# Turning exponentials with unit-matrix matmuls and the state by DMA, in an attention and Fourier-mix kernel

## The chip, the cores and the metric

The kernel runs on one core of one Trainium2 chip. The metric is device time in microseconds of one execution, measured several times; a profile of one execution shows where the time goes.

PE is the matmul engine (PEld its weight loads), DVE the vector engine, ACT the scalar engine, POOL is GpSimd, SP the sync engine whose queue issues most DMAs.

## The reference, cut to what matters

```python
# x: (8, 8, 512, 64) = batch, head, row, d;   state: (8, 8, 32, 64)
scores  = x @ state.T / 8;   a  = softmax(scores);   xread = a @ state      # 512 rows per head
scores2 = state @ x.T / 8;   a2 = softmax(scores2);  sread = a2 @ x         # 32 rows per head
attn    = concat([xread, sread], axis=2)            # 544 rows; heads are laid side by side
mixed   = real(fft over rows, then over d_model)    # 544 x 512 per batch
u       = attn + mixed
out     = u + relu(layer_norm(u) @ w_ch1) @ w_ch2   # 512 -> 2048 -> 512
```

The two score matrices are transposes of each other. The kernel needs their exponentials in two layouts: E has rows of x on partitions and feeds the state's reads; ET has states on partitions and feeds the reads of x. (The softmax goes without subtracting the maximum; the sums come from columns of ones.)

## The kernel before

A batch runs in three stages that are woven with those of its neighbours. In stage b the two MLP layers of batches b and b-1 give PE its bulk; batch b+1 makes its reads and its Fourier transform, and batch b+2 its scores. The parts that the change touches:

```python
def load_state(lo, hi):                    # partitions: (head of 4, state)
    nc.sync.dma_start(out=stf[:, lo:hi]..., in_=state[lo:hi].rearrange("b (g hh) j d -> (hh j) (b g) d", hh=4))

load_state(0, 1); load_x(0); load_state(1, B); load_x(1)

def more_loads():                          # on GpSimd, in this order
    ...
    nc.gpsimd.tensor_tensor(gate, xs_of[0][:, :, 0], w1[:, :, 3 * 512], op=ALU.add)
    load_x(2)                              # SP queue, follows the gate
    state_blocks(2, B, nc.gpsimd.tensor_copy)        # spreads the state of batches 2 to 7 into stb
    nc.gpsimd.tensor_copy(gate, xs_of[2][:, :, 0])   # waits for x of batch 2
    for q in range(4):
        nc.gpsimd.dma_start(out=w2[...], in_=w2v[...])   # second weights
# ---- cut ----
def turn_state():                          # sT = the state with d on partitions
    p = qt("sTp", BF16)
    for pr in range(4):
        g, hp = pr // 2, pr % 2
        nc.tensor.transpose(p[:, pr * 128:(pr + 1) * 128], sb[:, g, 4 + 128 * hp:132 + 128 * hp], ident)
    nc.vector.tensor_copy(sT, p[:, 0:512]...)        # ScalarE for batches 0 and 1

def scores_t(g):                           # states on partitions
    p = qt("eTp")
    for lo, hi, src in ((0, NM, slice(0, NM)), (NM, S, slice(S - 1, NM - 1, -1))):   # NM = 288, S = 512
        for hp in range(2):
            nc.tensor.matmul(p[:, lo:hi], lhsT=sT[:, 2 * g + hp, :], rhs=xT[:, 2 * g + hp, src], ...)
    nc.scalar.activation(ET[:, g, :], p, AF.Exp, scale=scale)

def scores(i):                             # rows on partitions, 64 columns per matmul, state backwards
    ...
    nc.scalar.activation(E[:, 2 * i:2 * i + 2]..., p, AF.Exp, scale=scale)

def fold_early():                          # batches 0 and 1 only: part of the fold on GpSimd
    fold_low(True, nc.gpsimd); next(fold_rows(slice(0, 1), nc.gpsimd)); fold_low(False, nc.gpsimd)
def fold():                                # the rest on VectorE, ending in the four XQ
    ...
# ---- cut: from batch 3 on x is turned by DMA; the order of a batch's score steps is ----
first = ([] if b >= x_by_dma else [turn_state, turn_x 0, turn_x 1]) + [scores_t(0), scores_t(1), scores(0), scores(1)]
# from batch 3 on turn_state stands first
```

The softmax here doesn't subtract the row's maximum and nothing guards it: scores larger than these inputs give would overflow.

## Time and profile before

| | before |
|---|---|
| time, median of 4 runs | 323.83 us (323.62 to 323.89) |
| span of the profiled execution | 322.0 us |
| PE / DVE / ACT / POOL busy | 95 / 59 / 45 / 22 % |
| PE busy from 80 to 260 us | 99.1 % |

The prediction below shows the views that say what bounds the kernel. First, two groups that the change removes, from the list of groups (line, engine, operation, tiles, shapes, count, then busy us, mean ns, idle time before and what ended it):

```profile
L362 PE MATMUL eTp<-xT,sT 128*128 128x288 bf16 (+1 forms) x64 | 9.6, 273 | 0.1
...
L338 DVE COPY sT<-sTp 128x512 bf16<-128x512 bf16 x6 | 2.5, 425 | 14.3 <-PE sTp L337 14.3
```

The 273 ns of a score matmul is its time from start to end. Matmuls overlap in the pipeline, so its price on a busy PE is read from the chain in order of time (0.44 us for four), not from this mean.

Second, GpSimd between 30 and 51 us, from its timeline (start, length, instruction):

```profile
30.77 3.42 POOL L147 CAST stb<-gen 32x768 bf16<-32x768 f32 x4
34.26 0.26 POOL L294 COPY gate<-xs 128x4 f32<-128x4 f32 x1
34.47 3.04 POOL L296 DMA_DIRECT2D w<-in_moe_w_ch_dram  x4
...
43.21 0.66 POOL L427 TENSOR_TENSOR XE<-XL 32x256 f32<-32x256 bf16 x1 [2.23 <-DVE XL L399]
...
46.20 0.72 POOL L430 TENSOR_TENSOR XO<-XL 32x255 f32<-32x255 bf16 x1
50.34 0.19 POOL L735 CAST gate<-XQ 128x1 f32<-128x1 bf16 x1 [3.42 <-DVE XQ L451]
```

It spreads the state, issues the second weights, and does its part of batch 1's fold (sums and differences of mirrored rows, called Sm, XE, XO and XQ, which the Fourier transform takes as input), for which it waits 2.23 us. At 50.34 us it passes the gate (a small copy made only to wait for something) behind which it casts x of batch 2. Third, two of VectorE's steps in the same fold, a sum Sm and the first XQ:

```profile
45.95 0.45 DVE L434 TENSOR_TENSOR Sm<-XF,XR 128x514 bf16<-128x514 bf16 x1
...
47.38 0.56 DVE L446 TENSOR_TENSOR XQ<-XE 128x384 bf16<-128x384 f32 x1
```

### The profile page before, as it was taken

The numbers are of one execution on the slowest core, as the hardware profiler recorded it, in microseconds if no ns is written. First come the engines' busy times: TensorE is split into PE (matmuls) and PEld (weight loads), VectorE is DVE, ScalarE is ACT, GpSimd is POOL, SyncE is SP. The second block draws the span as 40 slices with busy tenths as digits, with TensorE's granted clock in tenths as the row PEclk, the third lists the DMA queues.
The fourth block names the chain that finished last, engine by engine and source line by source line (L and its number), as shares of the span: only waits on it lengthen the run. The fifth ranks groups of instructions, "written<-read, shape, count | busy, mean of one in ns | idle before, by whom it ended". The sixth has DMA issues, their size and how long they took to land.

```text
span 322.0 us, 5748 instructions
## 1 busy us (share of the span) xinstructions
PE 305.8 (95%) x2183; PEld 179.9 (56%) x2214; DVE 190.5 (59%) x456; ACT 146.2 (45%) x283; POOL 72.1 (22%) x165
## 2 busy tenths in 40 slices
PE   5879999899999999999999999999999999999995
PEld 5758986455555555545645555545554544455444
DVE  8697576678767693782806864596747683100112
ACT  6798764845444344334453434434443422243200
POOL 7559952500240030300320024001300030000000
PEclk9999999999999999999999999999999999999999
DMA  7999994337556715275343423630252015302055
GB/s 142 215 201 167 196 196 85 51 95 150 111 115 155 133 33 130 65 142 108 76 90 77 105 64 83 130 67 33 74 92 65 35 33 130 81 35 65 36 124 138
DMA packets 107085, 33.17 MB, mean 103 GB/s; under 512 B 98481, under 2 KB 102833, under 8 KB 107057
## 3 DMA queue, kind: packets, MB, share of 16 engines
q1 hardware_dynamic: 96336, 27.03, 39.5%
q0 software_dynamic: 4224, 4.19, 8.1%
q10 hardware_dynamic: 6496, 1.57, 2.4%
q8 instruction: 17, 0.28, 0.4%
q14 instruction: 12, 0.09, 0.1%
HBM read 22.04 MB, written 13.63 MB: 111 GB/s over the span
## 4 chain that ended last, share of the span: by engine, by line
PE 78%; DVE 13%; ACT 3%; issue 2%; DMA 2%; POOL 1%; SPq 0%; DVEq 0%; ACTq 0%; POOLq 0%
PE po L699 31%; PE ph L633 29%; PE gp L513 3%; PE ph L643 2%; DMA xs<-in_x_dram 2%; PE eTp L362 2%; PE srp L409 2%; DVE U L483 2%; DVE st L306 1%; PE yp L479 1%; DVE XR L399 1%; PE po L691 1%; PE xrp L390 1%; PE yp L478 1%; PE esp L373 1%
## 5 line engine op out<-in xcount | busy, mean ns | idle before, releaser
L699 PE MATMUL po<-w,hT 128*128 128x512 bf16 x477 | 122.8, 379 | 0.8
L633 PE MATMUL ph<-unT,w 128*128 128x512 bf16 x438 | 113.8, 379 | 1.8 <-DVE ot L664 1.0
L635 ACT ACTIVATE hT<-ph 128x512 bf16<-128x512 f32 x112 | 66.8, 597 | 104.2 <-PE ph L633 104.1
L633 PEld LDWEIGHTS <-w 128*128 128x128 bf16 x576 | 51.1, 98 | 48.2 <-issue 1.7
L699 PEld LDWEIGHTS <-hT 128*128 128x128 bf16 x496 | 47.9, 98 | 45.7
L664 DVE SCALAR_TENSOR_TENSOR ot<-po,rstd,U 128x512 f32<-128x512 f32 (+1 forms) x33 | 24.2, 732 | 58.6 <-PE po L699 47.0
L523 POOL COPY GL<-G 128x128 bf16<-128x128 bf16 x8 | 2.4, 299 | 122.8 <-ACT G L521 122.8
L306 DVE BATCH_NORM_STATS2 st<-U 128x6 f32<-128x512 f32 x32 | 21.8, 682 | 0.1
L311 POOL TENSOR_TENSOR rstd<-rstd,mhalf 128x1 f32<-128x1 f32 x34 | 20.3, 598 | 2.7
L420 ACT ACTIVATE XR<-srp,rcs 32x64 bf16<-32x64 f32 x36 | 11.1, 309 | 20.8 <-DVE rcs L411 20.2
L310 POOL TENSOR_TENSOR rstd<-mv,epst 128x1 f32<-128x1 f32 x34 | 6.5, 191 | 61.5 <-DVE mv L308 61.5
L719 PE MATMUL warm<-ident 128*128 128x128 bf16 x182 | 14.5, 232 | 3.5 <-POOL ident masks.py:199 3.4
L521 ACT CAST G<-gp 128x288 bf16<-128x288 f32 x31 | 12.1, 396 | 12.2 <-PE gp L513 6.2
L643 PE MATMUL ph<-unT,w 128*128 128x128 bf16 x256 | 16.2, 219 | 0.2 <-ACT unT L557 0.2
L643 PEld LDWEIGHTS <-w 128*128 128x128 bf16 x256 | 15.2, 98 | 0.6 <-issue 0.3
L719 PEld LDWEIGHTS <-ident 128*128 128x128 bf16 x182 | 12.7, 104 | 4.2 <-POOL ident masks.py:199 3.4
L483 DVE TENSOR_TENSOR U<-yp,XR 128x512 f32<-128x512 f32 x16 | 10.9, 682 | 6.0 <-PE yp L479 5.9
L513 PEld LDWEIGHTS <-XQ 128*128 128x128 bf16 x96 | 8.6, 98 | 8.9 <-DVE XQ L446 3.4
L131 POOL CAST xin<-xs 128x2048 bf16<-128x2048 f32 x7 | 13.2, 1891 | 0.0
L547 DVE TENSOR_SCALAR ub<-U,mv 128x512 bf16<-128x512 f32 x24 | 12.3, 512 | 1.1 <-DVE mv L308 0.3
L390 PEld LDWEIGHTS <-ET 128*128 128x128 bf16 x80 | 7.2, 98 | 9.2 <-DVE XL L399 0.8
L399 DVE TENSOR_TENSOR XR<-xrp,rs 128x512 bf16<-128x512 f32 x16 | 11.1, 695 | 0.7
(175 smaller groups left out, 373.6 us busy)
## 6 DMA issues: line engine op xcount, KB each, us to landing
xs<-in_x_dram SPq DMA_DIRECT2D x30, 256.0 KB, 4.7
w<-in_moe_w_ch_dram POOLq DMA_DIRECT2D x8, 512.0 KB, 10.8
out_dram<-ot SPq DMA_DIRECT2D x15, 256.0 KB, 2.3
r_dram<-ot SPq DMA_DIRECT2D x14, 256.0 KB, 2.2
out_dram<-r_dram SPq DMA_DIRECT2D x14, 256.0 KB, 3.6
xs<-in_x_dram ACTq DMA_DIRECT2D x2, 256.0 KB
l_dram<-ot SPq DMA_DIRECT2D x2, 256.0 KB, 2.0
r_dram<-ot ACTq DMA_DIRECT2D x2, 256.0 KB
```

What stands on the lines that cost most here:

```text
L131: nc.gpsimd.tensor_copy(t[:, :, 1:513], xs)
L306: nc.vector.bn_stats(st6, u)
L311: nc.gpsimd.tensor_tensor(rstd, rstd, mhalf, op=ALU.pow)
L399: nc.vector.tensor_tensor(ov, in0=p[ps, :, 0:256].rearrange("p g (h d) -> p g h d", d=D), in1=rs[ps].unsqueeze(3).to_broadcast([n, 2, 4, D ...
L483: nc.vector.tensor_add(u.rearrange("p (k r) -> p k r", r=2), p.rearrange("p (r k) -> p k r", r=2)[:, 0:u.shape[1] // 2, :], x.rearrange("p ...
L513: nc.tensor.matmul(p[:, 0:NM], lhsT=XQ[:, j, c, :], rhs=tab[c], start=(c == 0), stop=(c == 2 and j != 2))
L633: nc.tensor.matmul(ph[:, o:o + n], lhsT=w1[:, c, f * 128:(f + 1) * 128], rhs=un_of[key][:, c, :], start=(c == 0), stop=(c == DC - 1))
L635: nc.scalar.activation(hT[:, per * i:per * i + per, :].rearrange("p a b -> p (a b)"), ph, AF.Relu, scale=-1.0 if key in flipped else 1.0)
L643: nc.tensor.matmul(ph[:, o:o + 128], lhsT=w1[:, c, f * 128:(f + 1) * 128], rhs=un_of[key][:, c, 128 * r:128 * r + 128], start=(c == 0), st ...
L664: nc.vector.scalar_tensor_tensor(ot[:, cols], in0=po_of[i][:, 0:cols.stop - cols.start], scalar=rstd, in1=u[:, cols], op0=ALU.mult, op1=AL ...
L699: nc.tensor.matmul(po_of[i], lhsT=h_of[key][:, f, i * 128:(i + 1) * 128], rhs=w2[:, f, :], start=(f == 0), stop=(f == FC - 1))
L719: nc.tensor.matmul(t[:, 0:128], lhsT=ident, rhs=ident, start=(i == 0), stop=(i == n - 1))
```

## The change

ET is no longer computed by score matmuls of its own, from batch 2 on. E, already exponentiated, is multiplied from the left into unit matrices, which turns it: a block of 128 rows becomes 128 columns. A mirrored unit matrix gives the backward order that rows 288 to 511 have in ET. ScalarE then copies instead of exponentiating. E carries each head's states backwards, so ET's partitions come out backwards as well and the state must lie backwards too: it is copied to DRAM with its rows reversed and reloaded from there ("the detour"). From batch 3 on, two DMA transposes turn the state instead of PE and VectorE.

```diff
@@ -48,6 +48,7 @@
     NL = 32
 
     r_dram = nc.dram_tensor("r_dram", (B, 2, 128, dm), F32, kind="Internal")
+    s_dram = nc.dram_tensor("s_dram", (B, H, Ns, D), F32, kind="Internal")
     l_dram = nc.dram_tensor("l_dram", (B // 4, 4, NL, dm), F32, kind="Internal")
     singles = ctx.enter_context(tc.tile_pool(name="singles", bufs=1))
 
@@ -80,10 +81,14 @@
     nc.gpsimd.iota(li[:, 128:256], pattern=[[2, 128]], base=2, channel_multiplier=0)
     nc.gpsimd.iota(li[:, 256:384], pattern=[[2, 128]], base=1, channel_multiplier=0)
     make_identity(nc, ident)
+    mirror = singles.tile([128, 128], BF16, name="mirror")
     nc.gpsimd.memset(halfpi, PI / 2)
     nc.gpsimd.memset(mhalfpi, -PI / 2)
     nc.gpsimd.memset(epst, eps)
     nc.gpsimd.memset(mhalf, -0.5)
+    nc.gpsimd.memset(mirror, 0.0)
+    nc.gpsimd.affine_select(out=mirror, in_=mirror, compare_op=ALU.not_equal, fill=1.0, base=-127,
+                            pattern=[[1, 128]], channel_multiplier=1)
 
     sg = singles.tile([128, 5], F32, name="sg")
     nc.gpsimd.tensor_copy(sg[:, 0:1], pi_[:, 3:4])
@@ -99,10 +104,10 @@
 
     stf = gen2[:, 1024:2048].rearrange("p (b g d) -> p b g d", b=B, g=2)
 
-    def load_state(lo, hi):
+    def load_state(lo, hi, src=state):
         nc.sync.dma_start(
             out=stf[:, lo:hi].rearrange("p b g d -> p (b g) d"),
-            in_=state[lo:hi].rearrange("b (g hh) j d -> (hh j) (b g) d", hh=4),
+            in_=src[lo:hi].rearrange("b (g hh) j d -> (hh j) (b g) d", hh=4),
         )
 
     xin_bufs = [singles.tile([128, 4, 514], BF16, name=f"xin{i}") for i in range(2)]
@@ -132,8 +137,11 @@
 
     load_state(0, 1)
     load_x(0)
-    load_state(1, B)
+    load_state(1, 2)
     load_x(1)
+    nc.sync.dma_start(out=s_dram[2:].rearrange("b h j d -> (b h) j d"),
+                      in_=state[2:, :, ::-1, :].rearrange("b h j d -> (b h) j d"))
+    load_state(2, B, s_dram)
     for i in range(2):
         nc.vector.memset(xin_bufs[i][:, :, 0:514:513], 1.0)
 
@@ -331,6 +339,10 @@
         Sm = wk.tile([128, 2, 514], BF16, name="Sm", tag="Sm", bufs=1)
 
         def turn_state():
+            if b >= x_by_dma:
+                for g in range(2):
+                    nc.sync.dma_start_transpose(out=sT[:, 2 * g:2 * g + 2, :], in_=sb[:, g, 4:260])
+                return
             p = psF.tile([128, 1024], BF16, name="sTp", tag="c") if b == 1 else qt("sTp", BF16)
             for pr in range(4):
                 g, hp = pr // 2, pr % 2
@@ -373,9 +385,17 @@
                     nc.tensor.matmul(
                         p[:, o:o + 64].rearrange("p (h j) -> p h j", j=Ns),
                         lhsT=xT[:, pr, si * 128:(si + 1) * 128],
-                        rhs=sT[:, pr, 64 * hp:64 * hp + 64].rearrange("p (h j) -> p h j", j=Ns)[:, :, ::-1],
+                        rhs=sT[:, pr, 64 * hp:64 * hp + 64].rearrange("p (h j) -> p h j", j=Ns)[:, :, ::-1 if b < 2 else 1],
                         start=True, stop=True)
             nc.scalar.activation(E[:, 2 * i:2 * i + 2].rearrange("p a b c -> p (a b c)"), p, AF.Exp, scale=scale)
+
+
+        def turn_scores(g):
+            p = qt("eTp")
+            for si, o, rhs in ((0, 0, ident), (1, 128, ident), (2, 256, ident[:, 0:32]),
+                               (2, 416, mirror[:, 0:96]), (3, 288, mirror)):
+                nc.tensor.matmul(p[:, o:o + rhs.shape[1]], lhsT=E[:, si, g, :], rhs=rhs, start=True, stop=True)
+            nc.scalar.copy(ET[:, g, :], p)
 
 
         def xread(c0, rev, name, o, ps=slice(0, 128), apart=False):
@@ -450,15 +470,15 @@
             nc.vector.tensor_sub(XQ[:, 2], XO[:, :, 0:128], XO[:, :, 256:128:-1])
             nc.vector.tensor_add(XQ[:, 3], XO[:, :, 128:0:-1], XO[:, :, 128:256])
 
-        first = ([] if b >= x_by_dma else [turn_state, lambda: turn_x(0), lambda: turn_x(1)]) + [
-            lambda: scores_t(0),
-            lambda: scores_t(1),
-            lambda: scores(0),
-            lambda: scores(1),
-        ]
-        if b >= x_by_dma:
-            turned[b] = lambda: (turn_x(0), turn_x(1))
-            first.insert(0, turn_state)
+        if b < 2:
+            first = [turn_state, lambda: turn_x(0), lambda: turn_x(1), lambda: scores_t(0), lambda: scores_t(1),
+                     lambda: scores(0), lambda: scores(1)]
+        else:
+            first = [lambda: scores(0), lambda: scores(1), lambda: turn_scores(1), lambda: turn_scores(0)]
+            if b >= x_by_dma:
+                turned[b] = lambda: (turn_x(0), turn_x(1), turn_state())
+            else:
+                first = [turn_state, lambda: turn_x(0), lambda: turn_x(1)] + first
         second = [
             lambda: xread(256, True, "xrp", XR[:, 0, 1:513]),
             sread,
```

## The prediction

> **What bounds the kernel now.** I read the views from coarse to fine: the page's busy shares, busy time by stretch, the chain that ended last in order of time, then the single groups. The page comes first: the total line and two of its 40-slice rows, each digit a tenth of a slice.
>
> ```profile
> PE 305.8 (95%) x2183; PEld 179.9 (56%) x2214; DVE 190.5 (59%) x456; ACT 146.2 (45%) x283; POOL 72.1 (22%) x165
> ...
> PE   5879999899999999999999999999999999999995
> ...
> PEclk9999999999999999999999999999999999999999
> ```
>
> The matmul engine is busy 95% of 322 us, with the clock fully granted, so no throttle stands in the way. A mean over stages can mislead, so I cut the span. The columns are: stretch, its length, then busy us of PE, PEld, DVE, ACT, POOL with counts, the clock, the DMA share and GB/s.
>
> ```profile
> 50.00:60.00 10.00, 9.21 (x74) 5.86 (x74) 6.80 (x23) 4.91 (x9) 3.76 (x7) 1.00 0.56 105
> 60.00:70.00 10.00, 9.04 (x67) 4.94 (x66) 5.47 (x16) 6.18 (x14) 3.30 (x5) 1.00 0.08 28
> 70.00:80.00 10.00, 9.26 (x50) 4.78 (x51) 8.29 (x19) 4.86 (x10) 0.00 (x0) 1.00 0.74 158
> 80.00:100.00 20.00, 19.90 (x124) 10.89 (x125) 13.42 (x33) 10.15 (x20) 5.31 (x10) 1.00 0.57 113
> 100.00:120.00 20.00, 19.84 (x110) 10.76 (x112) 15.93 (x35) 8.20 (x16) 2.67 (x7) 1.00 0.56 113
> ```
>
> From 80 to about 255 us PE is idle only 0.5% of the time (0.1 us in 20): a matmul taken out there shortens the run by what it cost. From 50 to 80 us PE has 2.5 us of gaps, so there another engine sets the pace. The kernel works in stages, one per batch; batch b+2's scores are made in the second half of stage b. So batch 2's are made at 56 to 64 us (loose), those of batches 3 to 7 in the dense part. Which engine paces the loose stretch, and what the touched groups cost, I take from the chain in order of time (start, length in us, what):
>
> ```profile
> 31.61 0.89 PE ph L643 x16
> ...
> 60.18 0.72 ACT ub L545
> ...
> 61.86 0.63 ACT ub L545
> 62.53 0.40 PE tp L556 x4
> ...
> 80.23 0.22 PE sTp L337 x4
> ...
> 83.92 0.44 PE eTp L362 x4
> ...
> 89.10 0.23 PE esp L373 x8
> ```
>
> At 60 to 62.5 us the chain runs over ScalarE's centring and PE waits for it. The other lines are prices in a dense stream: 16 matmuls of 128 columns 0.89 us, so 55.6 ns each; the four state transposes of a batch 0.22 us; one half of the scores with states on partitions (four matmuls, 288 and 224 columns twice) 0.44 us; eight 64-column score matmuls 0.23 us, 29 ns each although each brings its own weights.
>
> **What the Trainium skill says.** "TensorE: Matmul & The Clock Gate", section "Wait — 56ns, not 53.3ns?", has a warm matmul start every N / 2.4 GHz plus about 2.5 ns, and never faster than about 25 ns. The trace agrees: that gives 55.8 ns for 128 columns (55.6 seen), 29.2 for 64 (29 seen), and 2 x 122.5 + 2 x 95.8 = 437 ns for the half (0.44 seen). So reversed reading costs nothing here, and the formula prices the new matmuls. The same page, "Step-by-step: what each phase is for", says weight loads are pulled ahead of running matmuls; the 29 ns confirm it, so one weight load per new matmul is no limit. "VectorE: DVE Perf Modes", section "The three transpose paths", gives 1309 ns for a 128x128 DMA transpose; here a 128x512 one holds the sync queue 1.26 us and lands 2.5 us after issue, so for a transpose I use the trace. "DMA: Bandwidth & Descriptors", section "Two DMAs through the same engine are not ordered", explains why the reload of the reversed state must wait for the copy; no run shows that wait yet.
>
> **The change part by part.**
> 1. *Scores with states on partitions, batches 2 to 7.* Removed per batch: 2 x 0.44 = 0.88 us of PE. Added per batch: two groups of matmuls of E against a unit or mirrored unit matrix, of 128, 128, 32, 96 and 128 columns. Estimate from that TensorE page's formula: 3 x 55.8 + 25 + 42.5 = 235 ns, twice 0.47 us. Net 0.41 us per batch.
> 2. *State transposes by DMA, batches 3 to 7.* PE loses 0.22 us per batch: 5 x 0.22 = 1.1 us. DVE loses five copies of 425 ns, 2.1 us. DVE is busy 59%, so I credit this with nothing.
> 3. *ScalarE.* Two exponentials of 128x512 (592 ns each) become two copies of the same shape. The page has copies and relus of 128x512 at 586 to 597 ns: no change.
> 4. *Sync queue.* Two more DMA transposes per batch, 128x256 each. At the 128x512 price, an upper limit, 2.5 us more in a queue that has mostly waits.
> 5. *Prologue.* A memset (0.21 us) and a select (0.29 us) on GpSimd, which later idles 1.98 us before the sine tables: absorbed. State of batches 2 to 7 (384 KB) goes to DRAM reversed, then is reloaded. At about 200 GB/s this is 2 us extra of DMA. The DMA is quiet at 25.5 us, and GpSimd spreads that state from 30.8 us, so about 5 us are free. Hidden.
>
> What lies on the path: for batch 2, three of the four old score groups run before 62.5 us, where PE waits for ScalarE anyway, and the last is exchanged for one of the same length (0.23 for 0.24 us). So batch 2 gives nothing. Batches 3 to 7 give 5 x 0.41 + 1.1 = 3.15 us. I put 0.3 us against it for small new waits. 323.85 - 3.15 + 0.3 = **321.0 us**, 0.9% less.
>
> **The rivals.**
> *A new wait takes the gain's place.* The reads now need scores, exponential, turning matmul and copy in a row. The steps are laid 1/8 of a stage apart, 4.2 us of a 34 us stage, against about 1 us for an exponential with its waits. After the last turning matmul two 0.86 us steps follow before the read, against about 0.8 us for the copy. Only after stage 0 is there a single such step: at most 0.2 us lost. Each such wait, were it real in five stages, costs 0.3 us: total 322.5 at worst.
> *The state's DMA transposes come too late.* The sync queue in stage 1:
>
> ```profile
> 71.02 5.27 SPq L343 DMA_TRANSPOSE xT<-xin  x4
> 76.34 4.12 SPq L122 DMA_DIRECT2D xs<-in_x_dram  x5
> ```
>
> The two new transposes would follow at 76.3 and be down by 80 us (2 x 1.26 issued, the last 2.5 us to land from 77.6). Batch 3's first score step stands at 0.56 of stage 1 (old steps at 0.55 and 0.65 ran at 80.2 and 83.9), so at about 80.6: 0.6 us to spare. If they are late PE stops once, for 1 to 2 us: 322 to 323. In later stages the slack is 3 us or more (x transposes of stage 2 end at 100 us, scores due about 112).
> *DVE or the prologue gives more than counted.* DVE waits head-of-line for the state transposes, 14.3 us in five waits. If the work behind it was held up, its removal shortens the waits near 76, 139 and 256 us, where the chain runs over DVE. But those stretches come before or long after the copies. If I am wrong, and batch 2's 0.4 us also counts, 319.7 to 320.3.
> *The prologue slips:* if the reload is 5 us later than I think, the second weights come late and 1 to 4 us return. The 5 us of slack speak against it.
>
> **Range and chances.** Full gain with batch 2 and a little from DVE: 319.7. Gain with one late transpose or a small wait per stage: 322.4. So 319.7 to 322.4. The 2% line lies at 317.4, almost twice the gain that I can find on PE; slower by 2% (330.3) would need a wait of 1.5 us in every stage or more. Faster 0.03, within 2% 0.95, slower 0.02.
>
> **What would show it.** PE busy down by about 3.5 us (6 x 0.41 + 1.1). A turning group 0.24 us long in the chain where 0.44 stood. ScalarE's busy time the same within 1 us, DVE's down by 2 us. PE still 99% busy after 80 us, and the same gaps near 76 and 255 us. It is wrong if 50 to 64 us became shorter too (batch 2 not hidden), if PE stands before scores near 80 us for a DMA, if reads wait for the copied exponentials, or if the spreading of the state starts later than 30.8 us.

## The result, and the profile after

| | before | after |
|---|---|---|
| time, median of 4 runs | 323.83 us (323.62 to 323.89) | 321.61 us (320.86 to 321.77) |
| ratio to before | | 0.9928 (0.9911 to 0.9945) |
| span of the profiled execution | 322.0 us | 319.8 us |

A ratio is the mean time of one kernel's fast runs over that of the other's in the same rounds, so it is not quite the ratio of the medians. The change saves 2.2 us, 0.7%: the same within 2%, and inside the forecast range. Two things stand out. The best of its runs (320.86 us) gains 0.8 us more than the median does, and the runs spread over 0.9 us where those of before spread over 0.3.

The chain in order of time in stage 1 of the changed kernel (start, length, what):

```profile
80.83 0.86 PE po L719 x4
81.70 0.23 PE esp L385 x8
...
86.26 0.23 PE esp L385 x8
...
89.08 0.24 PE eTp L397 x5
...
91.91 0.24 PE eTp L397 x5
```

A turning group takes 0.24 us where a score group took 0.44. At 81.70 the first scores follow a layer-2 group without a gap: the state's DMA transposes came in time. PE's busy time by stretch, with the same columns as in the prediction:

```profile
50.00:60.00 10.00, 8.75 (x78) 5.36 (x76) 6.84 (x23) 4.82 (x9) 3.76 (x7) 1.00 0.71 127
60.00:70.00 10.00, 8.99 (x70) 5.11 (x68) 5.97 (x16) 5.85 (x13) 3.30 (x5) 1.00 0.08 28
70.00:80.00 10.00, 9.21 (x50) 4.49 (x48) 8.37 (x19) 4.99 (x10) 0.00 (x0) 1.00 0.57 118
80.00:100.00 20.00, 20.00 (x129) 10.86 (x128) 13.00 (x32) 10.70 (x21) 5.46 (x10) 1.00 0.72 139
```

The loose stretch has become looser and the dense one has stayed dense. To see where the time went I follow one event through the stages: the first matmul of the state's reads ("srp") in the chains of both kernels, with two events ahead and two behind. Times are us from the start of the span; the last column is the best kernel of the experiments (the run "The same, turning from batch 3 on only"), explained there.

| event | before | after | after - before | best |
|---|---|---|---|---|
| last read of batch 1 (xrp) | 44.55 | 44.35 | -0.20 | 44.47 |
| first transform of batch 2 (gp) | 76.49 | 77.10 | +0.61 | 76.42 |
| srp of batch 3 | 94.11 | 94.09 | -0.02 | 93.41 |
| srp of batch 4 | 128.44 | 127.79 | -0.65 | 127.11 |
| srp of batch 5 | 170.26 | 168.98 | -1.28 | 168.30 |
| srp of batch 6 | 204.16 | 202.25 | -1.91 | 201.57 |
| srp of batch 7 | 238.05 | 235.52 | -2.53 | 234.84 |
| last VectorE instruction | 318.72 | 316.19 | -2.53 | 315.50 |
| end of span | 322.0 | 319.8 | -2.2 | 318.7 |

From 77 us on each of the five batches saves 0.62 to 0.63 us. But 0.8 us are lost between the reads of batch 1 and the transform of batch 2. Where, the sync queue and GpSimd tell. First the queue's waits in the changed kernel (who waited for what: us, times, longest):

```profile
SPq L108 <- DMA s_dram<-in_state_dram: 14.9, 1, 14.9
```

And its timeline (start, length, instruction):

```profile
11.54 0.64 SPq L142 DMA_DIRECT2D s_dram<-in_state_dram  x1
27.15 0.38 SPq L108 DMA_DIRECT2D gen<-s_dram  x1
27.77 26.22 SPq L127 DMA_DIRECT2D xs<-in_x_dram  x12
```

The queue stands until the reversed copy has landed, at 27.1 us. Only then come the reload and, behind it, x of batch 2. GpSimd's timeline, to be held against the one of before:

```profile
31.26 3.53 POOL L155 CAST stb<-gen 32x768 bf16<-32x768 f32 x4 [0.63 <-DMA gen<-s_dram]
37.16 0.19 POOL L302 COPY gate<-xs 128x4 f32<-128x4 f32 x1 [2.37 <-DMA xs<-in_x_dram]
37.61 3.04 POOL L304 DMA_DIRECT2D w<-in_moe_w_ch_dram  x4 [0.27 <-issue]
...
44.20 0.66 POOL L447 TENSOR_TENSOR XE<-XL 32x256 f32<-32x256 bf16 x1
...
45.08 1.16 POOL L454 TENSOR_TENSOR Sm<-XF,XR 128x514 bf16<-128x514 bf16 x1
...
47.46 0.66 POOL L450 TENSOR_TENSOR XO<-XL 32x255 f32<-32x255 bf16 x1
50.94 0.19 POOL L755 CAST gate<-XQ 128x1 f32<-128x1 bf16 x1 [2.83 <-DVE XQ L471]
```

The spreading waits 0.63 us for the reload, the gate 2.37 us for x of batch 2; the second weights go out 3.1 us later, and the fold starts 1.0 us later and no longer waits for VectorE. It now meets VectorE's Sm and XQ:

```profile
45.75 0.77 DVE L454 TENSOR_TENSOR Sm<-XF,XR 128x514 bf16<-128x514 bf16 x1
...
47.50 1.04 DVE L466 TENSOR_TENSOR XQ<-XE 128x384 bf16<-128x384 f32 x1
```

The first XQ takes 1.04 instead of 0.56 us and Sm 0.77 instead of 0.45: both lie on the chain, and 0.48 + 0.32 us are the whole 0.8 that is lost. The Trainium skill, "SBUF — State Buffer", section "SBUF: two separate sides", calls the port that GpSimd and VectorE share an exclusive lock: a VectorE instruction with two SBUF inputs and a GpSimd one that reads SBUF do not run together, the later one blocks. The traces agree: GpSimd's XO runs from 47.46 to 48.12, XQ started at 47.50 and ended 0.42 us after it, and in two more runs below (the changed kernel again, the reversed detour alone) a slowed XQ also ended 0.42 us after XO. GpSimd's Sm runs from 45.08 to 46.24, and VectorE's ended 0.28 us after it. An undisturbed XQ takes 0.56 us and an undisturbed Sm 0.45, so by these records a little of each was done before the lock came free. The lock itself no run took away; what the runs change is the overlap.

The remaining 0.3 us are at the very end: from the last VectorE instruction to the end of the span it is 3.3 us before and 3.6 after. That is the landing of the last store.

### The profile page after: what moved, and what is told of

The parts are those of the page before. It is cut to its first block, busy times and chain, and to the rows that moved or that the text cites. A ratio compares the mean times of both kernels' runs of the same rounds, so it can differ in the third digit from the quotient of the medians.

```text
span 319.8 us, 5768 instructions
## 1 busy us (share of the span) xinstructions
PE 304.9 (95%) x2206; PEld 177.8 (56%) x2206; DVE 189.1 (59%) x451; ACT 145.8 (46%) x283; POOL 73.1 (23%) x167
## 4 chain that ended last, share of the span: by engine, by line
PE 79%; DVE 14%; ACT 3%; issue 2%; POOL 1%; DMA 1%; DVEq 0%; POOLq 0%; ACTq 0%
PE po L719 31%; PE ph L653 29%; PE gp L533 3%; PE warm L739 2%; PE ph L663 2%; PE srp L429 2%; DVE U L503 2%; DVE st L314 1%; PE yp L499 1%; DVE XR L419 1%; DVE ot L684 1%; PE yp L498 1%; PE xrp L410 1%; DVE XQ L466 1%; PE xfp L410 1%
## 5 line engine op out<-in xcount | busy, mean ns | idle before, releaser
L719 PE MATMUL po<-w,hT 128*128 128x512 bf16 x496 | 125.0, 379 | 0.0
L739 PE MATMUL warm<-ident 128*128 128x128 bf16 x182 | 15.4, 241 | 3.5 <-POOL ident masks.py:199 3.4
L739 PEld LDWEIGHTS <-ident 128*128 128x128 bf16 x182 | 13.6, 110 | 4.2 <-POOL ident masks.py:199 3.4
L663 PEld LDWEIGHTS <-w 128*128 128x128 bf16 x256 | 15.2, 98 | 0.6 <-issue 0.3
```

Source lines behind the costliest of these rows:

```text
L663: nc.tensor.matmul(ph[:, o:o + 128], lhsT=w1[:, c, f * 128:(f + 1) * 128], rhs=un_of[key][:, c, 128 * r:128 * r + 128], start=(c == 0), st ...
L719: nc.tensor.matmul(po_of[i], lhsT=h_of[key][:, f, i * 128:(i + 1) * 128], rhs=w2[:, f, :], start=(f == 0), stop=(f == FC - 1))
L739: nc.tensor.matmul(t[:, 0:128], lhsT=ident, rhs=ident, start=(i == 0), stop=(i == n - 1))
```

## The experiments

Eleven kernels ran, all correct, each with a profile and five rounds beside the kernel before (323.69 to 323.84 us, median).

**The changed kernel again.**

> The changed kernel itself, for pairing with the others on this chip. 321.6 us, and a spread of about 1 us where the kernel before has 0.3 us. My theory (the detour of the state through DRAM blocks the sync queue, and 0.6 us of the gain is lost before 77 us) expects a spread that comes from when the copy lands.

Measured: 321.96 us, six runs from 320.70 to 323.27. The spread is 2.6 us. The profiled run was the fastest, 320.70 us: there the queue waited 14.5 us for the copy, the first XQ took 0.77 us, and cast and gate before batch 2 were at 50.1 us, as early as before. GpSimd and VectorE met at other instructions there: Sm took 0.43 us, and VectorE's XE 0.43 where the kernel before has 0.78, which pays for the slower XQ. So in one execution the detour costs nothing early, in another 0.8 us. The slow ones, by their times, lose more than 2 us; none of them was profiled, so where they lose it is not shown.

**The copy issued earlier.** Edit:

```diff
     load_state(1, 2)
+    nc.sync.dma_start(out=s_dram[2:]..., in_=state[2:, :, ::-1, :]...)
     load_x(1)
-    nc.sync.dma_start(out=s_dram[2:]..., in_=state[2:, :, ::-1, :]...)
     load_state(2, B, s_dram)
```

> The changed kernel with one DMA moved: the copy of the state to DRAM is issued ahead of the five loads of x of batch 1 instead of behind them, so that it lands before the first weights crowd the DMA engines. The same bytes move. Theory A (the sync queue stood 14.9 us at the copy's completion, so the reload, x of batch 2 and the second weights came 3 us late, and GpSimd's share of the fold ran into VectorE's): the 14.9 us wait falls below 5 us, VectorE's first XQ of batch 1 takes 0.56 us again instead of 1.04 us, and the time is 321.0 us, 0.6 us less than the changed kernel. Theory B (the additional bytes cost the 0.6 us wherever they are): 321.6 us. If the earlier copy delays x of batch 1 too much: 322 us or more.

Measured: 322.23 us (320.87 to 322.61): a miss as a cure. The queue's wait for the copy did vanish and XQ took 0.56 us, as theory A has it. But x of batch 1 came too late instead. GpSimd's timeline of this run:

```profile
25.63 1.90 POOL L136 CAST xin<-xs 128x2048 bf16<-128x2048 f32 x1 [1.31 <-DMA xs<-in_x_dram]
```

Its cast waits 1.31 us for the data, and the reads of batch 1 start at 36.43 instead of 35.13 us. The reload was issued by 15.2 us here, so the same reversed copy was down at most 7.4 us after its issue: how long it takes depends on its place among the other loads. The detour has no free place ahead of x of batch 1 either.

**The detour alone, not reversed.** The kernel before, with the state of batches 2 to 7 copied to DRAM and reloaded in its old order.

> The kernel before with the detour alone: state of batches 2 to 7 copied to DRAM (not reversed) and reloaded, at the places of the changed kernel; everything else as before. Theory (the detour costs 0.6 to 0.8 us in the prologue, whatever the rest): 324.4 to 324.6 us against 323.8 us. Rival (the loss before 77 us comes from batch 2's new order of scores and reads, not from the detour): 323.8 us.

Measured: 323.57 us, ratio 0.9996 (0.9984 to 1.0008), runs within 0.5 us. By its letter this refuted the theory. But the copy was not the same one: unreversed rows join into large pieces. The queue's waits of this run:

```profile
SPq L104 <- DMA s_dram<-in_state_dram: 6.6, 1, 6.6
```

The count of packets says it too: 48 more than before on the sync queue's ring, against 1568 for the reversed copy (each count less the other parts of its kernel). So bytes through DRAM are free here; the next run asks after the rows.

**The detour alone, reversed.** As above, with `state[2:, :, ::-1, :]`; `scores` reads the state forwards from batch 2 on.

> The kernel before with the detour as the changed kernel has it, reversed rows and all (the plain copy of the run before had 48 packets, the reversed one has 1568); scores of batches 2 to 7 read the state straight instead of backwards to stay correct, all else as before. Theory (the row-wise reversed copy takes 15 us to land, so the reload, x of batch 2 and the second weights are late by an amount that differs from run to run): the sync queue waits about 14.5 us for the copy, the median is 324.3 to 325.0 us and the runs spread over 1 us or more. Rival (the detour is harmless, as the plain one was, and the spread of the changed kernel comes from its longer path of scores, exps, turning and reads): 323.8 us with a spread of 0.4 us.

Measured: 324.24 us, six runs from 323.52 to 326.27, mean 0.7 us above before. The queue waited 14.7 us. Old scores, old state transposes, and yet the spread of the changed kernel: the reversed, row-wise copy makes it. The median is at the theory's lower edge, and the interval of the ratio (0.9997 to 1.0044) just includes no change; the spread of 2.75 us is what tells.

**State by DMA alone.** The kernel before with the new `turn_state`, no detour, old scores.

> The kernel before with one part alone: from batch 3 on the state is turned by DMA, scores as before, no detour. Theory (PE pays, one for one, 5 x 0.22 us): 322.7 us, 1.1 us less than before. Rival (VectorE's 2.1 us of copies and its head-of-line waits also count): 321.9 us or less. Rival (DMA transposes are late and PE waits): 323.3 us or more.

Measured: 322.26 us (322.15 to 322.28), 1.5 us less than before: more than the theory. By the events of the table it saves 0.22 or 0.23 us in stages 1, 2, 4 and 5 and 0.43 in stage 3, 1.3 us in all. In stage 3 the new order lets scores run where PE waited for ScalarE's relu. A further 0.2 us was there before any changed instruction; profiles of one and the same kernel differ by 0.3 us at that point. VectorE's copies show nowhere in these events, though the median lies a little nearer to the rival's 321.9 us than to the theory's 322.7.

**No detour: a second exponential.** The state is loaded as before; ScalarE writes the exponentials a second time with the states in forward order, and the turning reads that copy.

```diff
+            if b >= 2:
+                nc.scalar.activation(E2[...].rearrange("p a g (h j) -> p (a g h) j", j=Ns)[:, :, ::-1],
+                                     p.rearrange("p (x j) -> p x j", j=Ns), AF.Exp, scale=scale)
-    lhsT=E[:, si, g, :]
+    lhsT=E2[:, si, g, :]
```

> The changed kernel without the detour: the state is loaded as before in one DMA, and ScalarE writes a second, unreversed copy of the exponentials from the same PSUM tile, from which the matmuls turn (12 more ScalarE instructions of 0.6 us, 7.2 us of an engine that is busy 45%). Theory (3.15 us from PE in batches 3 to 7, detour as the only loss): 320.5 to 320.8 us, spread 0.4 us or less. Rival (the new order itself costs in the loose stretch): 321.2 us or more, or a spread of 1 us.

Measured: 320.89 us, runs from 320.82 to 320.93, ratio 0.9909 (0.9896 to 0.9922). The spread is gone with the detour. The median is 0.1 us above the range that I had expected; the next run shows why.

**The same, turning from batch 3 on only.** `if b < 2` becomes `if b < 3` in the order of steps, and the second exponential starts at batch 3.

> As the run with two exps, but batch 2 makes its scores as the kernel before does; turned exps from batch 3 on. Theory (batch 2's scores stand where PE waits for ScalarE and VectorE, so turning them is worth nothing): the same within 0.15 us. Rival (batch 2's 0.41 us counts like the others'): 0.4 us slower than that run.

Measured: 320.48 us (320.46 to 320.72), ratio 0.9899 (0.9884 to 0.9913): 0.4 us *faster* than with batch 2. Neither theory had that. The chain of the run before, in stage 0, explains it:

```profile
58.61 0.48 ACT E L387
59.09 0.49 ACT E L389
59.58 0.48 ACT unT L577
60.07 0.72 ACT ub L565
```

In this run the chain lies on ScalarE from 57.8 us on, and the second exponential of batch 2 (L389) stands in it; in the kernels before and after it lies on VectorE until about 60 us. That cost belongs to my workaround, not to the change. For the change itself the table and the gates shown above answer: from the gate of batch 2's cast to the first transform of batch 2 it is 76.49 - 50.34 = 26.15 us before and 77.10 - 50.94 = 26.16 us after. Turning batch 2 is worth nothing.

**A late reload.** The detour for batches 3 to 7 only, batch 2 as before; the reload is issued behind x of batch 3, and GpSimd spreads that state after it has cast x of batch 2, at 52 us.

> The changed kernel with batch 2 scored as before from a state loaded straight, and the detour for batches 3 to 7 only, its reload issued behind x of batch 3 and spread by GpSimd after x of batch 2 is cast. Same bytes, but nothing early waits for the copy any more. Theory: 320.6 us, spread 0.4 us, as the run with two exps. Rival (the bytes of the detour cost wherever they lie, or GpSimd's spreading at 53 us slows VectorE in the loose stretch): 321.0 us or more.

Measured: 320.95 us (320.80 to 321.35). XQ took 0.56 us, and every event up to the last VectorE instruction (315.42 us) is where the best kernel has it. So the reversed copy's bytes (320 KB here, five batches of the six) cost nothing on the way; what cost was to stand in line ahead of x of batch 2 and the second weights. The end of the span, though, came 3.6 us after the last VectorE instruction, as in every profile of the changed kernel and of the earlier copy. The kernel before and all other runs have 3.1 to 3.3 us. Those three kernels alone have both the reversed copy and the turning; what delays the last landing is open.

**State turned by PE again, in the best kernel.**

> The best version so far (two exps, turned scores from batch 3 on, no detour, 320.48 us) with one part undone: the state of batches 3 to 7 is turned by PE and copied by VectorE as in the kernel before. Theory (five times 0.22 us of PE and nothing else): 321.6 us, 1.1 us more. Rival (VectorE's five copies and head-of-line waits count too, as the 1.55 us of the run with the state DMA alone may say): 322.0 us or more.

Measured: 321.89 us (321.57 to 322.05), 1.4 us more than the best kernel on the same chip (below). By the events the five stages cost 0.22 to 0.24 us each, 1.13 us; the rest, against the profile of the table's last column, is in the start and the landing of the last store. The theory holds in the trace. The median alone would not decide: it lies 0.3 us above the theory and 0.1 us below the rival's 322.0.

**Every turning matmul twice.** `for _ in range(2):` around the matmul of `turn_scores`.

> The best version so far (320.48 us) with each turning matmul of batches 3 to 7 issued twice; the second writes the same values again. Measures the price of the turning itself. Theory (a group costs 0.24 us and lies on the path one for one): 5 x 2 x 0.24 = 2.35 us more, 322.8 us. Rival (part of the turning hides in gaps of PE): less than 2 us more. Rival (weight loads of E limit the group): more than 2.6 us more.

Measured: 322.84 us (322.59 to 322.97), 2.34 us more than the best kernel, against 2.35 expected. The chain has the doubled groups:

```profile
88.40 0.47 PE eTp L398 x10
...
91.46 0.47 PE eTp L398 x10
```

So 0.235 us per group, and each lies on the path in full.

**The best kernel again.**

> The best version so far again, on the same chip as the two runs that start from it: 320.5 us, spread 0.4 us or less.

Measured: 320.50 us (320.36 to 320.78), ratio 0.9898 (0.9883 to 0.9913). Turned exponentials and state by DMA from batch 3 on, without the detour, beat both the kernel before (by 3.3 us) and the changed kernel (by 1.1 us, the difference of the medians 321.61 and 320.50; the two did not share a chip).

## Why the prediction was right or wrong

The time (321.61 against 321.0 us) lay in the range, the class was right, and the main mechanism was shown.

- **PE bounds, and pays one for one: right.** Five batches saved 0.62 to 0.63 us each, where 0.41 + 0.22 = 0.63 had been predicted. The doubled turning and the undone state DMA measure both terms apart: 0.235 us per group, as the formula of the Trainium skill's "TensorE: Matmul & The Clock Gate", section "Wait — 56ns, not 53.3ns?", had it (235 ns), and 0.22 to 0.24 us per batch.
- **Batch 2 gives nothing: right.** 26.15 and 26.16 us over the stretch.
- **ScalarE unchanged, VectorE uncredited: right.** ScalarE is busy 146.2 us before and 145.8 after. VectorE fell by 1.4 us, not 2; the slowed XQ and Sm gave 0.8 back.
- **"Hidden" for the prologue: wrong.** This is the step that failed. I allowed 2 us for additional bytes at 200 GB/s and saw 5 us of slack. What counted was how long the copy takes in rows of 256 bytes at that place in the queue (14.5 to 14.9 us from wait to landing), and that the in-order queue keeps x of batch 2 waiting meanwhile. I had the sign among the rivals (spreading later than 30.8 us: it was 31.3), but spoke against it. It cost 0.8 us in the profiled run and nothing in the other; over all ten runs of the changed kernel the mean is 321.7 us, 1.2 us above that of the best kernel. The landing of the last store is 0.3 us of it.
- **0.3 us for small new waits: right by chance.** No read waited for the turned exponentials in a way that cost, and no new wait appeared in the dense stages. The reserve stood for a loss elsewhere.
- **The state's DMA transposes in time: right.** Two of them held the queue 1.24 us each, the upper limit that I had used, and landed 2.3 us after issue; scores at 81.7 us did not wait.
- **"PE busy down by about 3.5 us": no test.** The page shows 305.8 and 304.9 us. But the trace of before lacks more matmul records (477 of 496 in the layer-2 group that the other trace has in full), so the two sums do not compare. The events do.
- **Small slips of reading.** From 80 to 260 us PE is idle 0.9%, not 0.5%: 140 to 160 us alone has 0.73 us, where the chain runs over VectorE. The 2% line is a little over twice the 3.15 us of gain away, not almost twice. Neither changes the forecast.

## What to carry to other kernels

On an engine that is 99% busy, price a change from the chain in order of time, in start-to-start costs, and expect it one for one; where the engine has gaps, expect nothing. Before trusting that a transfer is hidden, ask how many rows it has and what stands behind it in the same in-order queue: here 384 KB in large pieces cost nothing, and in small rows about 0.7 us in the mean. And when a changed kernel's runs spread wider than before, look for a race of transfers in the prologue, for a single profile may fall on the lucky side.

## What the Trainium skill lacked or had wrong

- "DMA: Bandwidth & Descriptors" gives a size below which a transfer loses line rate, and an overhead per small packet, but no time for a DRAM-to-DRAM copy in small rows beside other loads: 384 KB in 256-byte rows made its queue wait 14.5 to 14.9 us, the same bytes in large pieces, at the same place, 6.6 us.
- "VectorE: DVE Perf Modes", section "The three transpose paths", has one figure, 1309 ns for a 128x128 DMA transpose. Here a 128x256 one holds the sync queue 1.24 us and a 128x512 one 1.26 us: for these two sizes it is a time per instruction, hardly dependent on size. That page gives no second size.
- "SBUF — State Buffer", section "SBUF: two separate sides", has the later of two instructions that want the shared port fully blocked. Here a blocked XQ ended 0.42 us after GpSimd's XO in three traces, where it takes 0.56 us alone: by the records some 0.14 us of it was not held up (spans on GpSimd are rough).
